# Opening of a fused attention and maxout kernel: weight requests, vector copies and six product units put in another order

## The chip, the cores and the metric

The kernel runs on one core of a Trainium2 chip. The core has engines with a queue of instructions each, worked through in order: TensorE (PE, matrix products and transposes; its weight loads are shown as PEld), VectorE (DVE), ScalarE (ACT), GpSimd (POOL) and SyncE (SP), which only requests transfers. Transfers between device memory and on-chip memory run on 16 DMA engines; here SyncE and GpSimd request nearly all of them, and a request of GpSimd may convert fp32 to bf16 on the way. An engine waits for another one through semaphores. The metric is device time in microseconds of one execution; the profile records one execution in detail.

## What is computed

There are B = 8 batches with H = 8 heads, S = 576 tokens and head size D = 64, and 16 beacon keys and values per head that stand ahead of the ordinary ones. Attention is causal on the ordinary keys and open on the beacons:

```
k_all, v_all = concat([beacon_k, k]), concat([beacon_v, v])     # 592 keys
scores = (q @ k_all.T) / sqrt(64), future ordinary keys masked
a = exp(scores - max); a /= a.sum(-1) + 1e-9
x = (a @ v_all) as [4608 tokens, 512]
h = max(x @ w1, x @ w2, x @ w3)          # 512 -> 768
out = h @ w_out                          # 768 -> 512, fp32
```

## The kernel before, in words

**Attention.** Two heads make a pair; a batch has four pairs, so there are 32 pairs, 0 to 31. Two pairs make a quad. For each pair the queries and keys are turned by TensorE transposes (`turn`, L399, `turn_part`, L417) and copied from PSUM to `qT` and `kT`. Then a burst of score products follows (`emit_scores`, L488, or `emit_burst`, L522), in four groups; ScalarE takes the exponential of each group into `at_sb`. Masks set the future to zero: `emit_masks` (L540) does it on GpSimd (L553), or, with a third argument True, on VectorE (L551), by a product with the triangle `tri`. Then the products with the values and with a column of ones are formed per quad (`emit_pv`, L576, or `emit_pv_whole`, L616), the row sums are inverted on ScalarE (logarithm and exponential) and VectorE multiplies them in, which gives `xT` (L681 or L658), the transposed input of the second part.

**Maxout and output product.** Tokens are taken in 9 blocks of 512. The list `units` (L800 to L818) holds the work of all blocks in order. For the first block the products with w1 and w2 are twelve half units (`mm1_halves`, L733: two column tiles, 256 tokens), and those with w3 six units of 512 tokens (`mm1_unit`, L722). Then four output units follow (`mm2_unit`, L756). A unit whose entry is larger than `ready` may not be emitted yet: the half units of tokens 0 to 255 need nothing but the first half of batch 0, those of tokens 256 to 511 the rest of it. The copy or maximum behind a unit runs on VectorE (L754, L752, L729), or in part on ScalarE where a unit closes a stage. `F(n)` in the opening emits the next n units.

**What sets the order.** The whole order is written out by hand under a manual schedule: each call appends to the queues of the engines that it uses. `start` and `first_batch` (L910) write out batch 0, whose pairs are handled in halves of 288 tokens, `second_batch` (L998) handles pairs 4 to 7 with two or three units between the bursts, and the loop of `emit_all` (L1048) handles pairs 8 to 31. In that loop the number of units emitted by the end of a pair is given as an absolute count (L1054), so units that were not emitted earlier are caught up there.

**PSUM.** There are eight banks. In the first batch they have fixed roles: 0 to 3 for scores, 4 and 5 for turning and for values, 6 and 7 for units. From the turning of pair 4 on, `free_banks` is a list from which the bank that has been used least lately is taken; L992 sets it once.

**Transfers.** The first batch's queries and keys are requested at the start, most of them by GpSimd; its values by SyncE behind a gate, a tiny VectorE write (L291). `cast_first_v(t)`, written `V(t)`, converts the t-th of five value tiles on GpSimd (L332). `load_w(i, gs)` lets GpSimd request halves of weight array i (L342). `load_cast(p)` lets GpSimd request the queries and keys of pairs 4 to 9 (L256). For later batches SyncE requests fp32 data (`load_pair`, L218, `load_v`, L288) and GpSimd converts them (L275, L320); `next_load` takes the next ones of a list.

In `first_batch`, `S_` stands for `emit_scores`, `T` for `turn_part`, `M` for `emit_masks`, `P` for `emit_pv`.

Of the kernel before, what the change touches and what calls it, by code (L numbers as in the profile page):

```python
# [17 lines left out]
def kernel(  # L18
# [22 lines left out]
    n_ft = d_ff // 128  # L41
# [99 lines left out]
    free_banks = list(range(N_BANK))  # L141
# [63 lines left out]
    by_pool = nc.gpsimd.tensor_copy  # L205
# [102 lines left out]
    def cast_v(b, piece, cast):  # L308
        st = stage.pop(("v", b, piece))
        if b not in v_tiles:  # L310
            v_tiles[b] = v_pool.tile([128, n_kt, H, D], BF16, name="v_sb")
        v_sb = v_tiles[b]
        t_lo, t_hi = V_PIECES[piece]
        t = t_lo
        while t < t_hi:
            t1 = t + 1
            while t1 < t_hi and k_rows[t1] == k_rows[t]:
                t1 += 1
            n = k_rows[t]
            cast(  # L320
                v_sb[0:n, t:t1].rearrange("p t h d -> p (t h d)"),
                st[0:n, (t - t_lo) * H * D : (t1 - t_lo) * H * D],
            )
            t = t1
# [14 lines left out]
    def load_w(i, gs=range(n_quad)):  # L339
        wv = (moe_w1, moe_w2, moe_w3)[i].rearrange("(g p e) f -> g p e f", g=n_quad, e=2)  # L340
        for g in gs:
            nc.gpsimd.dma_start(out=w_in[i][:, 2 * g : 2 * g + 2], in_=wv[g])  # L342
# [6 lines left out]
    def load_beacons(b0, b1, dst, queue=None):  # L349
        for b in range(b0, b1):  # L350
            (queue or nc.sync).dma_start(
                out=dst[Nb * (b - b0) : Nb * (b - b0 + 1)],
                in_=beacon_k[b].rearrange("h n d -> n h d"),
            )

    def turn_beacons(b0, b1, src):
        n = Nb * (b1 - b0)
        ps = sc_psum.tile(BF16)[:, 0, 0 : PPB * n].rearrange("p (i n) -> p i n", i=PPB)
        for pi in range(PPB):
            nc.tensor.transpose(  # L360
                ps[:, pi],
                src[:, 2 * pi : 2 * pi + 2].rearrange("p h d -> p (h d)"),
                ident[0:n, 0:n],
            )
        if b0 == 0:
            by_act(kTs[0][:, 0:Nb], ps[:, 0, 0:Nb])
        by_act(bT[:, :, Nb * b0 : Nb * b1], ps)
# [43 lines left out]
    def fill(at_bank, n):  # L411
        for _ in range(n):
            nc.tensor.matmul(  # L413
                acc[:, at_bank], busy[:, 0:128], busy, start=True, stop=True
            )
# [29 lines left out]
    def place_beacons(p, copy):  # L445
        b, pi = divmod(p, PPB)
        copy(kTs[p % NT][:, 0:Nb], bT[:, pi, Nb * b : Nb * (b + 1)])
# [8 lines left out]
    def turn_pair(p, q_copy):  # L456
        banks = [next_psum(BF16)[:, 0:S] for i in range(2)]
        for i in range(2):
            turn(p, i, banks[i])
        evac_k(p, banks[1], by_dve)  # L460
        evac_q(p, banks[0], q_copy)
# [213 lines left out]
    def multiply(count=NPASS):  # L675
        for _ in range(min(count, len(products))):
            quad, hf, n, ps, recip = products.pop(0)
            b, g = divmod(quad, n_quad)
            c0 = b % RING * S + hf * HALF
            part, bank, lo, ca, cb = passes[hf][n]  # L680
            nc.vector.tensor_mul(  # L681
                xT[:, 2 * g + part - 1, c0 + ca : c0 + cb],
                ps[bank][:, lo : lo + cb - ca],
                recip[:, ca:cb],
            )
            if g == n_quad - 1 and n == NPASS - 1:
                ready[0] = 2 * b + hf
# [8 lines left out]
    MID = TOKB // 2  # L696
# [103 lines left out]
    units = []  # L800
    for tb in range(n_tokb):
        need = 2 * ((TOKB * (tb + 1) - 1) // S) + 1
        if tb == 0:
            order = [(lo, f, i) for i in range(2) for lo in (0, MID) for f in (0, 2, 4)]
            *order, last = order
            for lo, ft, i in order:
                units.append((need if lo else 0, mm1_halves, (tb, ft, i, lo, lo + MID)))
            for ft in range(n_ft):
                units.append((need, mm1_unit, (tb, ft, 2)))
            units.insert(len(order) + 2, (need, mm1_halves, (tb, last[1], last[2], last[0], last[0] + MID)))  # L810
        else:
            for ft in range(n_ft):
                for i in range(3):
                    units.append((need, mm1_unit, (tb, ft, i)))
        for tt in range(TOKB // 128):
            units.append((need, mm2_unit, (tb, tt)))
# [8 lines left out]
    def emit_ffn(limit, new_ps=ffn_psum.tile, close=False):  # L825
        if not may_emit(limit):
            return False
        need, fn, args = units[done[0]]
        done[0] += 1
        fn(*args, new_ps, *([True] if close else []))  # L830
        return True
# [26 lines left out]
    def next_load(n=1, **gate):  # L858
        for _ in range(n):
            if loads:  # L860
                loads.pop(0)(**gate)
# [42 lines left out]
    S_, T, M, P, V = emit_scores, turn_part, emit_masks, emit_pv, cast_first_v  # L904

    def F(n=1, new_ps=ffn_psum.tile, close=False):
        for _ in range(n):
            assert emit_ffn(END, new_ps, close)

    def first_batch():  # L910
        S_(0, 0)
        T(2, 0, 0, 6)
        T(3, 0, 0, 4)
        load_v(0, 0, nc.vector)
        load_v(0, 1)
        load_beacons(1, B_PE, bk32_1)
        S_(1, 0)
        T(2, 0, 1, 7)
        T(3, 0, 1, 5)
        S_(2, 0)  # L920
        T(0, 1, 0, 6, None, 2)
        T(1, 1, 0, 4)
        S_(3, 0)
        M(0, 0, True)
        M(1, 0, True)
        T(0, 1, 1, 7, None, 2)
        T(1, 1, 1, 5)
        S_(0, 1)
        T(2, 1, 0, 6, None, 2)
        T(3, 1, 0, 4)  # L930
        S_(0, 2)
        M(0, 1)
        M(2, 0, True)
        T(2, 1, 1, 7, None, 2)
        T(3, 1, 1, 5)
        S_(0, 3)
        M(0, 2)
        M(3, 0, True)
        S_(1, 1)
        M(0, 3, True)  # L940
        V(0)
        load_w(0, [0])
        fill(6, 2)
        S_(1, 2)
        M(1, 1)
        V(1)
        load_w(0, [1])
        S_(1, 3)
        M(1, 2)
        fill(6, 2)  # L950
        S_(2, 1)
        M(1, 3, True)
        V(2)
        fill(6, 2)
        S_(2, 2)
        M(2, 1)
        V(3)
        S_(2, 3)
        M(2, 2)
        V(4)  # L960
        load_w(1, [0])
        P(0, 0)
        S_(3, 1)
        M(2, 3, True)
        P(1, 0, apart=True)
        S_(3, 2)
        M(3, 1)
        S_(3, 3)
        M(3, 2)
        M(3, 3, True)  # L970
        load_w(1, [1])
        by_pool(bk16_1, bk32_1)
        load_cast(PPB)
        load_cast(PPB + 1)
        load_cast(PPB + 2)
        load_w(2)
        load_cast(PPB + 3)
        invert_sums()
        invert_sums()
        multiply()  # L980
        multiply()
        P(0, 1, tiles=sc_psum.tile())
        invert_sums()
        P(1, 1, tiles=sc_psum.tile())
        multiply()
        invert_sums()
        F(3)
        multiply()
        turn_beacons(1, B_PE, bk16_1)
        place_beacons(PPB, by_act)  # L990
        F(3)
        free_banks[:] = [4, 5, 0, 1, 2, 3, 6, 7]  # L992
        turn_pair(PPB, by_act)
        load_v(1, 0, nc.vector)
        load_v(1, 1)
        F(2, next_psum)

    def second_batch():  # L998
        for p in range(PPB, 2 * PPB):
            place_beacons(p + 1, by_act)  # L1000
            emit_burst(p)
            if p == PPB + 1:
                load_cast(2 * PPB)
            if p == PPB + 2:
                load_w_out()
                load_cast(2 * PPB + 1)
            for gi in range(NG):
                emit_masks(p, gi)
                if p == PPB + 2 and gi == 1:
                    cast_v(1, 0, by_pool)  # L1010
            if p == PPB + 2:
                cast_v(1, 1, by_pool)
                next_load(gate=nc.gpsimd)
                next_load(4)
            if p + 1 < 2 * PPB:
                turn_pair(p + 1, by_dve)
                F(2, next_psum)
                if p < PPB + 2:
                    F(1, last_pair(), True)
        F(2, next_psum)  # L1020
        finish = emit_pv_whole(n_quad)
        turn_pair(2 * PPB, by_dve)
        F(2, next_psum)
        finish()
# [93 lines left out]
```

## Time and profile before

| quantity | value |
| --- | --- |
| median of 3 runs | 288.97 us (288.5 to 290.31) |
| the profiled execution | 288.44 us |
| its span, first to last instruction | 286.7 us |
| granted TensorE clock, mean | 0.997 |
| busy: TensorE, VectorE, ScalarE, GpSimd | 274.8, 173.7, 160.0, 135.7 us |
| DMA traffic | 48.84 MB, mean 170 GB/s |

The times of the views count from the start of the span. A row of a timeline gives start and length of one or several equal instructions, the engine, the source line, the operation with target and source, shape and count; brackets hold the idle time of the engine before it and who ended it. Matmuls are pipelined, so several in a row take less than the sum of their single lengths. Some matmul records are missing, so that a count can be one or two short. A list of transfers gives, per request, size and time from request to landing.

### The profile page before, as it was taken

To read this page: it belongs to the slowest core of one execution; us is meant where nothing else is said; L and a number is where in the kernel's file an instruction comes from. 1 tells how busy PE (TensorE), PEld (TensorE's weight loads), DVE (VectorE), ACT (ScalarE), POOL (GpSimd) and SP (SyncE) were. 2 spreads that over 40 slices of the span, in tenths; PEclk is the share of its full clock that TensorE was granted. 3 is DMA by queue.
4 is the path that set the end of the run, shared out by engine and by line. 5 is a ranking of instruction groups with operands and counts; after the bars stand their busy time and mean duration, and the time that the engine had idled before them with its cause. 6 is when DMAs were issued, how large, how long until landed. Compare 5 with 4: busy or idle time off the path is not lost.

```text
span 286.7 us, 7740 instructions
## 1 busy us (share of the span) xinstructions
PE 274.8 (96%) x3042; PEld 156.9 (55%) x3073; DVE 173.7 (61%) x306; ACT 160.0 (56%) x299; POOL 135.7 (47%) x282
## 2 busy tenths in 40 slices
PE   7789899998999999999999999999999999999994
PEld 3447675554556555555556787455555554444442
DVE  4757776554683848373836383648363847876872
ACT  3796287698568595858585757666666640000000
POOL 7088269368477683648465836484436210000000
PEclk9999999999999999999999999999999999999998
DMA  8999999999994899999999999989853003003004
GB/s 142 201 153 140 207 208 170 246 200 313 268 188 127 236 267 195 184 234 257 260 209 202 245 237 242 196 177 232 179 139 114 0 2 133 16 1 146 2 0 146
DMA packets 85316, 48.84 MB, mean 170 GB/s; under 512 B 64416, under 2 KB 80032, under 8 KB 85280
## 3 DMA queue, kind: packets, MB, share of 16 engines
q1 hardware_dynamic: 78176, 42.22, 64.3%
q0 software_dynamic: 6544, 5.80, 13.8%
q8 instruction: 24, 0.39, 0.6%
q10 hardware_dynamic: 560, 0.33, 0.5%
q14 instruction: 12, 0.10, 0.2%
HBM read 35.13 MB, written 14.22 MB: 172 GB/s over the span
## 4 chain that ended last, share of the span: by engine, by line
PE 89%; DVE 3%; ACT 2%; POOL 2%; issue 1%; DMA 1%; SPq 0%; ACTq 0%; DVEq 0%
PE acc L711 44%; PE acc L763 16%; PE acc L635 11%; PE acc L513 8%; PE acc L740 4%; PE acc L602 2%; PE acc L404 2%; PE acc L466 1%; DMA out_dram<-y 1%; ACT at_sb L507 1%; PE acc L498 1%; POOL v_sb L320 1%; ACT at_sb L531 1%; PE acc L413 1%; PE acc L425 1%
## 5 line engine op out<-in xcount | busy, mean ns | idle before, releaser
L711 PE MATMUL acc<-xT,w_sb 128*128 128x512 bf16 (+4 forms) x720 | 134.5, 337 | 2.0 <-DVE xT L658 0.4
L553 POOL TENSOR_SCALAR_AFFINE_SELECT at_sb<-at_sb 128x256 bf16<-128x256 bf16 (+2 forms) x176 | 63.7, 383 | 91.4 <-ACT at_sb L531 80.4
L729 DVE TENSOR_TENSOR hT<-hT,acc 128x512 bf16<-128x512 bf16 x102 | 70.0, 687 | 59.6 <-PE acc L711 56.4
L711 PEld LDWEIGHTS <-w_sb 128*128 128x128 bf16 x744 | 69.1, 98 | 59.4 <-issue 0.2
L531 ACT ACTIVATE at_sb<-acc 128x208 bf16<-128x208 f32 (+3 forms) x140 | 89.6, 735 | 8.5 <-PE acc L513 7.3
L763 PE MATMUL acc<-w_out_sb,hT 128*128 128x512 bf16 (+2 forms) x241 | 48.2, 348 | 0.3
L275 POOL CAST p<-st 96x768 bf16<-96x768 f32 x44 | 35.0, 824 | 0.0
L763 PEld LDWEIGHTS <-hT 128*128 128x128 bf16 x246 | 22.6, 98 | 22.2 <-DVE hT L729 1.9
L770 DVE COPY y<-acc 128x512 f32<-128x512 f32 (+1 forms) x35 | 22.0, 628 | 20.9 <-PE acc L763 14.0
L731 ACT CAST hT<-acc 128x352 bf16<-128x352 f32 x18 | 8.1, 452 | 45.8 <-PE acc L711 45.8
L731 DVE CAST hT<-acc 128x512 bf16<-128x512 f32 (+1 forms) x48 | 26.6, 554 | 10.0 <-PE acc L711 9.8
L513 PE MATMUL acc<-qT,kT 64*128 64x208 bf16 (+1 forms) x336 | 26.7, 279 | 0.1
L788 ACT COPY y<-acc 128x320 f32<-128x320 f32 x1 | 0.4, 426 | 46.0 <-PE acc L781 46.0
L635 PE MATMUL acc<-at_sb,v_sb 128*32 128x512 bf16 (+5 forms) x672 | 23.0, 281 | 0.6 <-POOL v_sb L320 0.6
L513 PEld LDWEIGHTS <-kT 64*128 64x128 bf16 x336 | 15.2, 94 | 12.5 <-issue 2.6
L658 DVE TENSOR_TENSOR xT<-raw,recip 128x576 bf16<-128x576 f32 x28 | 21.1, 796 | 0.0
L635 PEld LDWEIGHTS <-v_sb 128*32 128x32 bf16 (+1 forms) x672 | 14.5, 96 | 7.8 <-POOL v_sb L320 1.2
L320 POOL CAST v_sb<-st 128x1536 bf16<-128x1536 f32 (+2 forms) x21 | 18.3, 896 | 0.0
L645 ACT COPY raw<-acc 128x512 f32<-128x512 f32 x28 | 15.8, 630 | 2.6 <-PE acc L635 2.3
L635 PE MATMUL acc<-at_sb,ones 128*32 128x512 bf16 (+3 forms) x336 | 14.9, 283 | 0.0
L507 ACT ACTIVATE at_sb<-acc 128x1024 bf16<-128x1024 f32 (+3 forms) x16 | 13.1, 864 | 3.3 <-PE acc L498 3.1
L740 PE MATMUL acc<-xT,w_sb 128*128 128x256 bf16 x96 | 11.8, 272 | 0.8 <-DVE xT L681 0.8
(73 smaller groups left out, 176.8 us busy)
## 6 DMA issues: line engine op xcount, KB each, us to landing
out_dram<-y SPq DMA_DIRECT2D x35, 256.0 KB, 3.5
st<-in_q_dram SPq DMA_DIRECT2D x22, 288.0 KB, 4.4
st<-in_k_dram SPq DMA_DIRECT2D x22, 288.0 KB, 5.0
st<-in_v_dram SPq DMA_DIRECT2D x24, 256.0 KB, 5.9
w_sb<-in_moe_w_dram POOLq DMA_DIRECT2D x6, 384.0 KB, 6.9
q_dram<-p SPq DMA_DIRECT2D x16, 144.0 KB, 2.3
k_dram<-p SPq DMA_DIRECT2D x16, 144.0 KB, 2.2
st<-in_v_dram SPq DMA_DIRECT2D x8, 224.0 KB, 5.8
```

The source lines that it names most:

```text
L275: cast(t16.rearrange("p r h d -> p h r d"), st[0:QP, i * NQ2 : (i + 1) * NQ2].rearrange("p (h r d) -> p h r d", h=2, r=QR),)
L320: cast(v_sb[0:n, t:t1].rearrange("p t h d -> p (t h d)"), st[0:n, (t - t_lo) * H * D : (t1 - t_lo) * H * D],)
L513: nc.tensor.matmul(ps, kTs[p % NT][hs, 128 * t : 128 * t + 128], qTs[p % NT][hs, q0:q1], start=True, stop=True, tile_position=(64 * e, 0),)
L531: nc.scalar.activation(out=both_heads(p, gi)[:, e0:e1], in_=acc[:, first + e0 : first + e1, 0 : g_width(p, gi)], func=AF.Exp, scale=scale,)
L553: nc.gpsimd.affine_select(out=view, in_=view, compare_op=ALU.is_ge, fill=0.0, base=x0, pattern=[[0, 2], [1, hi - lo]], channel_multiplier=-1,)
L635: nc.tensor.matmul(acc[32 * j : 32 * j + 32, bank, lo + q0 - qa : lo + qb - qa], lhsT, at_view(PPQ * quad + j // 2, t, j % 2, q0, qb), sta ...
L711: nc.tensor.matmul(ps[:, a:b], w_in[i][:, ct, 128 * ft : 128 * (ft + 1)], xT[:, ct, x0 : x0 + b - a], start=(ct == 0), stop=(ct == n_ct - 1),)
L729: nc.vector.tensor_max(h[:, lo:hi], h[:, lo:hi], ps[:, lo:hi])
L731: (by_act if hi < TOKB else by_dve)(h[:, lo:hi], ps[:, lo:hi])
L740: nc.tensor.matmul(ps, w_in[i][:, ct, 128 * (ft + f) : 128 * (ft + f + 1)], xT[:, ct, tb * TOKB + lo : tb * TOKB + hi], start=(ct == 0), s ...
L763: nc.tensor.matmul(ps[:, lo:hi], hT[:, ft, 128 * tt : 128 * (tt + 1)], w_out_sb[:, ft, lo:hi], start=(ft == 0), stop=(ft == n_ft - 1),)
L770: (by_act if hi < d_model else by_dve)(y[:, lo:hi], ps[:, lo:hi])
```

## The change

It edits three places. In `units`, the twelfth half unit is no longer moved behind two w3 units; the twelve stand in order. In `first_batch`, VectorE's masks of pairs 0, 1 and 2 (group 0) move behind the copies of the next transposes; the first four weight requests move ahead of their former places among GpSimd's masks and casts, the first one ahead of `V(0)`, and `V(0)` itself ahead of mask (0, 2); VectorE's multiplication of the second quad's second half follows one unit instead of three, pair 4 is turned behind five units instead of six, and one unit instead of two follows it. `free_banks` has its last two entries exchanged. So two units fewer have been emitted when pair 4's burst begins, and the absolute count in the loop catches them up at pair 9. In `second_batch`, five loads of SyncE, with their gate on GpSimd, move ahead of the second value cast of batch 1.

```diff
@@ units @@
         if tb == 0:
-            order = [(lo, f, i) for i in range(2) for lo in (0, MID) for f in (0, 2, 4)]
-            *order, last = order
-            for lo, ft, i in order:
-                units.append((need if lo else 0, mm1_halves, (tb, ft, i, lo, lo + MID)))
+            for i in range(2):
+                for n, lo in ((0, 0), (need, MID)):
+                    for ft in range(0, n_ft, 2):
+                        units.append((n, mm1_halves, (tb, ft, i, lo, lo + MID)))
             for ft in range(n_ft):
                 units.append((need, mm1_unit, (tb, ft, 2)))
-            units.insert(len(order) + 2, (need, mm1_halves, (tb, last[1], last[2], last[0], last[0] + MID)))
@@ first_batch @@
         S_(3, 0)
-        M(0, 0, True)
-        M(1, 0, True)
         T(0, 1, 1, 7, None, 2)
         T(1, 1, 1, 5)
         S_(0, 1)
+        M(0, 0, True)
         T(2, 1, 0, 6, None, 2)
         T(3, 1, 0, 4)
         S_(0, 2)
         M(0, 1)
-        M(2, 0, True)
+        load_w(0, [0])
+        M(1, 0, True)
         T(2, 1, 1, 7, None, 2)
         T(3, 1, 1, 5)
         S_(0, 3)
+        V(0)
         M(0, 2)
+        load_w(0, [1])
+        M(2, 0, True)
         M(3, 0, True)
         S_(1, 1)
         M(0, 3, True)
-        V(0)
-        load_w(0, [0])
         fill(6, 2)
         S_(1, 2)
         M(1, 1)
         V(1)
-        load_w(0, [1])
         S_(1, 3)
         M(1, 2)
+        load_w(1, [0])
         fill(6, 2)
...
         S_(2, 2)
         M(2, 1)
+        load_w(1, [1])
         V(3)
         S_(2, 3)
         M(2, 2)
         V(4)
-        load_w(1, [0])
...
         M(3, 3, True)
-        load_w(1, [1])
         by_pool(bk16_1, bk32_1)
...
         invert_sums()
-        F(3)
+        F()
         multiply()
+        F(2)
         turn_beacons(1, B_PE, bk16_1)
         place_beacons(PPB, by_act)
-        F(3)
-        free_banks[:] = [4, 5, 0, 1, 2, 3, 6, 7]
+        F(2)
+        free_banks[:] = [4, 5, 0, 1, 2, 3, 7, 6]
         turn_pair(PPB, by_act)
         load_v(1, 0, nc.vector)
         load_v(1, 1)
-        F(2, next_psum)
+        F(1, next_psum)
@@ second_batch @@
             if p == PPB + 2:
-                cast_v(1, 1, by_pool)
                 next_load(gate=nc.gpsimd)
                 next_load(4)
+                cast_v(1, 1, by_pool)
```

## The prediction

> **What bounds the kernel now.** I read the busy shares of the page first, then the gaps of TensorE in its timeline, then what stood before each gap on the other engines, and last the landings of the transfers.
>
> ```profile
> PE 274.8 (96%) x3042; PEld 156.9 (55%) x3073; DVE 173.7 (61%) x306; ACT 160.0 (56%) x299; POOL 135.7 (47%) x282
> ```
>
> TensorE is busy 274.8 of 286.7 us; no other engine passes 61%. Where its 11.9 us of idle time lie decides what an edit can win. One stretch of the view by windows (time, then busy us of PE, PEld, DVE, ACT, POOL, clock, DMA share, GB/s):
>
> ```profile
> 75.00:240.00 165.00, 163.97 (x1789) 95.71 (x1807) 96.27 (x153) 106.89 (x203) 88.68 (x180) 1.00 0.84 187
> ```
>
> From 75 to 240 us TensorE lacks 1.03 us in 165 and has the full clock. So a microsecond won or lost before 75 us goes straight to the end; the change edits only that part. The rows of TensorE's timeline there on which I rest (start, length, line, count, in brackets the idle time before and who ended it):
>
> ```profile
> 11.08 0.45 PE L425 MATMUL acc<-ident,quad 96*64 96x96 bf16 x12
> ...
> 12.46 0.26 PE L498 MATMUL acc<-qT,kT 64*128 64x208 bf16 x2 [0.70 <-DVE kT L433]
> ...
> 19.15 0.40 PE L602 MATMUL acc<-at_sb,ones 128*32 128x288 bf16 x12
> ...
> 22.25 0.68 PE L602 MATMUL acc<-at_sb,ones 128*32 128x288 bf16 x20 [0.54 <-ACT at_sb L507]
> ...
> 25.36 2.86 PE L740 MATMUL acc<-xT,w_sb 128*128 128x256 bf16 x24
> ...
> 28.36 0.39 PE L740 MATMUL acc<-xT,w_sb 128*128 128x256 bf16 x2
> ...
> 29.37 0.27 PE L740 MATMUL acc<-xT,w_sb 128*128 128x256 bf16 x1 [0.62 <-DVE xT L681]
> 29.80 2.52 PE L740 MATMUL acc<-xT,w_sb 128*128 128x256 bf16 x21 [0.16 <-DVE xT L681]
> ...
> 32.25 0.70 PE L404 MATMUL acc<-ident,quad 96*64 96x96 bf16 x24
> ...
> 53.39 2.76 PE L763 MATMUL acc<-w_out_sb,hT 128*128 128x512 bf16 x11
> ...
> 65.02 0.38 PE L711 MATMUL acc<-xT,w_sb 128*128 128x512 bf16 x1 [0.42 <-DVE xT L658]
> ...
> 70.49 0.83 PE L635 MATMUL acc<-at_sb,v_sb 128*32 128x512 bf16 x16 [0.33 <-POOL v_sb L320]
> ...
> 71.61 0.90 PE L635 MATMUL acc<-at_sb,v_sb 80*32 80x80 bf16 x24 [0.29 <-POOL v_sb L320]
> ```
>
> Four places: VectorE's key copy (0.70), VectorE's xT product (0.62 + 0.16), xT of the second batch (0.42), and GpSimd's value casts (0.33 + 0.29). No gap names a weight: unit 0 starts at 25.36 without one.
>
> **The change part by part.** *VectorE's copies ahead of the masks.*
>
> ```profile
> 10.94 1.09 DVE L551 TENSOR_TENSOR at_sb<-at_sb,tri 128x224 bf16<-128x224 bf16 x6
> 11.95 0.82 DVE L433 COPY kT<-acc 128x288 bf16<-128x288 bf16 x2
> ...
> 26.45 0.69 DVE L754 CAST hT<-acc 128x512 bf16<-128x512 f32 x1
> ...
> 28.26 0.69 DVE L754 CAST hT<-acc 128x512 bf16<-128x512 f32 x1 [0.25 <-PE acc L740]
> ...
> 28.87 0.88 DVE L681 TENSOR_TENSOR xT<-acc,recip 128x288 bf16<-128x288 f32 x3
> ...
> 54.24 0.75 DVE L440 COPY qT<-acc 128x576 bf16<-128x576 bf16 x1
> ```
>
> Six masks (1.09 us) stand before the key copy for which TensorE waits at 12.46. With the copies first, pair 0's can start when the first six of the twelve transposes of 11.08 are in: about 11.4, at the latest 11.53. It takes about 0.45 (two take 0.82), so TensorE resumes near 11.95: **0.5 us** won (0.4 to 0.7). The masks move behind into idle time of VectorE; the first is read by the value products at 19.15, so they cost nothing, unless VectorE were full there, and then 1.09 at most. The 0.5 carries on, since ScalarE's exponentials run gapless in the middle of the opening:
>
> ```profile
> 15.09 5.00 ACT L507 ACTIVATE at_sb<-acc 128x576 bf16<-128x576 f32 x7 [0.36 <-PE acc L498]
> ...
> 25.94 0.44 ACT L671 ACTIVATE recip<-recip 128x288 f32<-128x288 f32 x1
> ```
>
> Their first one waits for TensorE (0.36), so all seven start earlier with it. Their pace remains a floor: the 0.54 at 22.25 stays.
>
> *Weights between masks and casts.* The rows of GpSimd's timeline; then the landings (last number, us from issue) of the first and the fourth half of the first two weight arrays, of the last tile of the first values, and of pair 4's keys; then the DMA load (last two numbers) in two windows:
>
> ```profile
> 13.83 0.40 POOL L553 TENSOR_SCALAR_AFFINE_SELECT at_sb<-at_sb 128x256 bf16<-128x256 bf16 x1 [7.86 <-ACT at_sb L507]
> ...
> 15.62 0.57 POOL L342 DMA_DIRECT2D w_sb<-in_moe_w_dram  x1
> ...
> 18.46 0.68 POOL L332 CAST v_sb<-st 128x512 bf16<-128x512 f32 x1
> ...
> 22.54 0.55 POOL L342 DMA_DIRECT2D w_sb<-in_moe_w_dram  x1
> ```
>
> ```profile
> w_sb<-in_moe_w_dram POOLq DMA_DIRECT2D x1, 384.0 KB, 4.7
> ...
> w_sb<-in_moe_w_dram POOLq DMA_DIRECT2D x1, 384.0 KB, 7.7
> ...
> st<-in_v_dram SPq DMA_DIRECT2D x1, 160.0 KB, 5.2
> ...
> quad<-in_k_dram POOLq DMA_DIRECT2D x1, 144.0 KB, 7.2
> ```
>
> ```profile
> 15.00:16.00 1.00, 1.00 (x12) 0.38 (x7) 1.00 (x5) 0.92 (x2) 1.00 (x3) 1.00 0.84 181
> 16.00:17.00 1.00, 0.45 (x7) 0.19 (x4) 0.28 (x3) 1.00 (x2) 0.48 (x2) 1.00 0.78 113
> ```
>
> The first request moves from 15.62 to behind the mask of 13.83 (itself 0.5 earlier): about 13.7, so 1.9 us sooner. The others follow among the casts. TensorE waited for no weight, so they win nothing themselves. But the halves land one behind another: the first at 15.62 + 4.7 = 20.3, the fourth at 22.54 + 7.7 = 30.2, three steps of 3.3; and pair 4's keys, issued at 24.3, land right behind at 31.5. An earlier start moves the keys too: by 0 if the weights find no room beside the values, by 1.9 if they find it all. From 15 to 17 the DMA engines show 0.84 and 0.78, part of it free, so I take **1.1**, just over the middle: keys at 30.4. Three of the four requests (0.57 each) now stand before the third value cast, of 18.46, instead of two: with everything else 0.5 earlier that cast ends near 18.6 to 18.7. TensorE's value products start at 19.15 - 0.5 = 18.65 with the sums (0.40) and read it after them: hidden by these 0.4; without that cover, up to 0.57.
>
> *Five units ahead of pair 4, VectorE's product after the first unit.* Unit 3 of the first products needs xT of the second half of the tokens. ScalarE had its reciprocal at 26.38 (25.94 + 0.44), but VectorE put three casts of finished units before the three products of 28.87. From 28.36 to 32.32 units 3 to 5 take 3.96 us where units 0 to 2 took 2.86 (row of 25.36): 1.1 lost. Afterwards the products follow the first cast (26.45 + 0.69), end about 0.9 later, at 28.0 on the old scale, and unit 3 finds them done. What is late next: unit 3 needs the bank of unit 1, whose cast now ends at 28.0 + 0.69 = 28.7 against a start at 28.4. That is 0.3 lost, net **0.8 us** (0.3 to 1.1).
>
> Pair 4 is then turned at 32.25 - 0.95 (one unit, 2.86/3) - 0.5 - 0.8 = 30.0; the keys are read 0.35 later, at 30.35, and land at 30.4: **0.1 lost** (0 to 1.1). The burst of pair 4 follows after one unit; the key copy (as large as the 0.75 of 54.24) fits beside that unit's 0.95.
>
> *Two units later in the order from here.* The bursts of pairs 4 to 7 start two units earlier relative to the units, which costs TensorE nothing by itself. From pair 8 on the difference is two output units; eleven recorded matmuls of twelve take 2.76 at 53.39, so 2.8 us. They now stand between the bursts of pairs 9 and 10. So xT of the second batch is asked for 2.8 later after its product: the 0.42 of 65.02 goes. GpSimd's work behind the burst of pair 9 runs without a gap into the value casts:
>
> ```profile
> 67.43 1.59 POOL L275 CAST p<-st 96x768 bf16<-96x768 f32 x2
> 68.97 2.58 POOL L320 CAST v_sb<-st 128x1536 bf16<-128x1536 f32 x3
> ```
>
> With 2.8 us more between burst and use, they end before they are needed: 0.33 + 0.29 go. Together **1.0 us** (0 to 1.04). New: before the burst of pair 8 stand two first-layer units (0.95 each) instead of two output units, and VectorE, which turns pair 8's queries until 54.99 (54.24 + 0.75), casts them late; the last group of the burst needs the second one's bank: **0.2 lost** (0 to 0.5). The next loads moved ahead of the second value cast on GpSimd are asked for 1.2 us sooner relative to the casts and never waited for: 0 (0.3 either way).
>
> The sum: 0.5 + 0.8 - 0.1 + 1.0 - 0.2 = **2.0 us**. The profiled execution took 288.44 (span 286.7 and 1.7 around it): 286.4 by its scale. It lies 0.5 below the median of the runs shown, 288.97; the forecast for the median is 288.97 - 2.0 = **287.0**.
>
> **The rivals.** *Pair 4's keys take the place of the wait.* If the weights get no room beside the values, the keys still land at 31.5 and TensorE stands 1.1 at pair 4. For it: they land at a fixed place behind the weights, and TensorE comes 2.25 sooner. Against: the shares of 0.84 and 0.78. The gain shrinks by 1.05: 288.0.
>
> *The weights push out the last values (slower).* Which of two queues the DMA engines serve (packets, MB, share of 16 engines; q1 carries SyncE's requests, q0 GpSimd's): the microsecond from 13, that from 18, and that from 36, after a request of SyncE:
>
> ```profile
> q1 hardware_dynamic: 788, 0.20, 104.1%
> ...
> q0 software_dynamic: 63, 0.19, 100.4%
> ...
> q0 software_dynamic: 213, 0.20, 123.4%
> ...
> 33.81 0.31 SPq L299 DMA_DIRECT2D st<-in_beacon_v_dram  x1
> ```
>
> From 13 only values flow, 1.041 x 16 / 788 = 21 ns of an engine per packet; from 18 only weights, 255 ns each. The 0.84 of the window from 15 are then about 640 packets of values, 40 per engine, the last tile's, which was asked for at 12.5 and landed 5.2 later at 17.7. If an engine took one packet of each queue in turn, they would take 40 x 0.276 = 11 us while weights last (four times 3.3): landing near 26, cast near 26.7. TensorE wants it about 0.9 after 22.25 - 0.5, so 4.0 late; the gains past there (and the 0.1 at pair 4) stay: 288.97 - 2.0 - 0.1 + 4.0 = 290.9. It bites from a landing later than 22 and makes the kernel slower from 24. Against: the values asked for from 33.81 have no packet from 36 to 37, where 213 of q0, asked for earlier, are all that these two queues move. That looks like order of request, and this tile is asked for before the weights.
>
> [...]
>
> *It doesn't do what it says later.* The waits of 65.02 and 70.49 return at other places because the loads of the second batch are no sooner while TensorE is: gain 1.0, so 288.0.
>
> **How the numbers follow.** Forecast 0.63, keys late 0.14, later waits return 0.14, values pushed out 0.09. All terms at their best end (0.7 + 1.1 + 1.04 + 0.3) give 3.1 less: 285.8; both rivals of 288.0 together give 289.0. With a few tenths for the spread of a median the range is 285.6 to 289.3; the slower rival lies beyond it. About 1% (2.9 us) is what a measurement of this kernel can tell from no change: faster than that needs every term at its best (0.09), slower needs the slower rival at a third more than its price of 4.0 and little gained (0.06), within 0.85.
>
> **What would show it.** Right: TensorE's row of about 12.46 waits 0.2 or less; no wait of the first products for xT L681 and a short one for hT L754; pair 4's transposes start at about 30 and wait for their keys 0.3 at most; no wait for xT L658 or v_sb L320 near 65 and 70. Wrong: a TensorE or GpSimd wait for st between 18 and 23, a wait for the quad before pair 4 above 0.5, or 75 us on no longer gapless.

## The result, and the profile after

The changed kernel took 287.43 us in the median of eight runs (286.45 to 287.76), the kernel before 288.97 (288.5 to 290.31): the ratio is 0.9937, with the 95% interval 0.9916 to 0.9958. The forecast was 287.0, 2.0 less than before; 1.5 less were measured. The profiled execution took 286.92 with a span of 285.2, against 288.44 and 286.7. So the size is nearly that of the forecast, but the way to it is not: what stands ahead of the burst of pair 9 was to win 1.0 and lost 0.3, and what stands from there on was to win 1.0 and won 1.7.

The page of the changed kernel, its busy shares:

```profile
PE 275.9 (97%) x3073; PEld 157.4 (55%) x3073; DVE 176.6 (62%) x306; ACT 160.1 (56%) x299; POOL 136.5 (48%) x282
```

The long middle is as gapless as before, so that what happens ahead of 75 us still goes straight to the end (view by windows, columns as in the prediction):

```profile
75.00:240.00 165.00, 165.00 (x1809) 95.78 (x1808) 96.35 (x153) 106.67 (x201) 88.84 (x180) 1.00 0.87 187
```

TensorE's timeline of the changed kernel, the rows that answer to those of before:

```profile
12.16 0.26 PE L498 MATMUL acc<-qT,kT 64*128 64x208 bf16 x2 [0.20 <-DVE kT L433]
...
20.79 0.20 PE L602 MATMUL acc<-at_sb,ones 128*32 128x48 bf16 x2 [0.45 <-DVE at_sb L551]
...
22.58 0.68 PE L602 MATMUL acc<-at_sb,ones 128*32 128x288 bf16 x20 [0.76 <-ACT at_sb L507]
...
25.19 0.22 PE L602 MATMUL acc<-at_sb,ones 80*32 80x80 bf16 x4 [0.46 <-issue]
...
26.34 2.86 PE L740 MATMUL acc<-xT,w_sb 128*128 128x256 bf16 x24
...
29.57 1.91 PE L740 MATMUL acc<-xT,w_sb 128*128 128x256 bf16 x16 [0.16 <-DVE hT L754]
31.40 0.70 PE L404 MATMUL acc<-ident,quad 96*64 96x96 bf16 x24
...
33.87 0.38 PE L513 MATMUL acc<-qT,kT 64*128 64x336 bf16 x6 [0.17 <-DVE hT L754]
...
54.54 0.36 PE L513 MATMUL acc<-qT,kT 64*128 64x336 bf16 x5 [0.20 <-DVE hT L729]
...
60.53 0.92 PE L513 MATMUL acc<-qT,kT 64*128 64x208 bf16 x12
...
68.06 0.92 PE L513 MATMUL acc<-qT,kT 64*128 64x208 bf16 x12
...
71.16 1.04 PE L711 MATMUL acc<-xT,w_sb 128*128 128x512 bf16 x4
```

The wait for the key copy fell from 0.70 to 0.20, and yet unit 0 starts at 26.34 instead of 25.36. Three waits stand between that were not forecast: one for a mask of VectorE (0.45), a longer one for ScalarE (0.76 instead of 0.54), and one for nothing that the profile shows ("issue", 0.46). Not all of the 0.98 belongs to the change. VectorE's copy of the queries that precedes all that was edited starts 0.20 later too (VectorE's timeline, the kernel before and the changed one):

```profile
10.20 0.82 DVE L433 COPY qT<-acc 128x288 bf16<-128x288 bf16 x2 [0.84 <-PE acc L425]
...
10.40 0.82 DVE L433 COPY qT<-acc 128x288 bf16<-128x288 bf16 x2 [0.84 <-PE acc L425]
```

Such shifts differ from one execution to the next: this copy starts between 10.08 and 10.72 in the profiles of this case. Counted from it, unit 0 starts after 15.16 before and after 15.94 now, 0.78 later. From unit 0 to the turning of pair 4 the forecast holds. The points of the kernel before that the rest is compared with, from its timeline:

```profile
56.09 1.21 PE L513 MATMUL acc<-qT,kT 64*128 64x208 bf16 x12
...
62.93 0.92 PE L513 MATMUL acc<-qT,kT 64*128 64x208 bf16 x12
...
68.45 0.91 PE L513 MATMUL acc<-qT,kT 64*128 64x208 bf16 x12
...
72.53 1.04 PE L711 MATMUL acc<-xT,w_sb 128*128 128x512 bf16 x3
```

The burst of pair 9 (burst 9, at 62.93 before) starts 2.40 earlier, at 60.53, but the two output units that stood ahead of it are still to come. Two such units take 2.70 in the kernel before, from 53.39 (in the prediction) to the next row, burst 8 at 56.09. So the changed kernel is 0.3 behind here, 0.2 of it from the later start. From burst 9 to burst 10 (68.06, before 68.45) it needs 7.53 us instead of 5.52 with those 2.7 more in it: 0.7 won. From burst 10 to the unit after the value products it needs 3.10 instead of 4.08: 1.0 won. That makes 1.4 at 71.16, and the spans differ by 1.5.

### The profile page after: what moved, and what is told of

It reads as the page before. It is cut to its first block, busy times and chain, and to the rows that moved or that the text cites. A ratio compares the mean times of both kernels' runs of the same rounds, so it can differ in the third digit from the quotient of the medians.

```text
span 285.2 us, 7775 instructions
## 1 busy us (share of the span) xinstructions
PE 275.9 (97%) x3073; PEld 157.4 (55%) x3073; DVE 176.6 (62%) x306; ACT 160.1 (56%) x299; POOL 136.5 (48%) x282
## 4 chain that ended last, share of the span: by engine, by line
PE 91%; DVE 5%; ACT 1%; issue 1%; ACTq 0%; DVEq 0%
PE acc L711 46%; PE acc L763 16%; PE acc L635 11%; PE acc L513 8%; PE acc L740 3%; DVE at_sb L551 2%; PE acc L404 2%; PE acc L466 2%; PE acc L602 1%; ACT at_sb L531 1%; DVE kT L433 1%; DVE hT L754 1%; PE acc L425 1%; DVE qT L433 1%; PE acc L413 1%
## 5 line engine op out<-in xcount | busy, mean ns | idle before, releaser
L553 POOL TENSOR_SCALAR_AFFINE_SELECT at_sb<-at_sb 128x256 bf16<-128x256 bf16 (+2 forms) x176 | 64.5, 387 | 92.0 <-ACT at_sb L531 81.7
L763 PEld LDWEIGHTS <-hT 128*128 128x128 bf16 x246 | 22.6, 98 | 21.7 <-DVE hT L729 1.6
L451 DVE COPY kT<-acc 128x576 bf16<-128x576 bf16 x12 | 9.0, 753 | 5.7 <-PE acc L404 5.7
```

What stands on the lines that cost most here:

```text
L553: nc.gpsimd.affine_select(out=view, in_=view, compare_op=ALU.is_ge, fill=0.0, base=x0, pattern=[[0, 2], [1, hi - lo]], channel_multiplier=-1,)
L763: nc.tensor.matmul(ps[:, lo:hi], hT[:, ft, 128 * tt : 128 * (tt + 1)], w_out_sb[:, ft, lo:hi], start=(ft == 0), stop=(ft == n_ft - 1),)
```

## The experiments

Two theories of the late unit 0 stood after this profile. **Masks:** the masks, moved behind the copies, hold up VectorE, and the value products wait for them. **Weights:** the early weight requests delay something that TensorE needs, and the mask wait only hides it. Each experiment is told with its edit against the changed kernel, unless another one is named. The medians of the kernel before were 288.97 beside the first four kernels, 288.85 beside the next four and 289.0 beside the last four.

### 1. All masks of VectorE's first group ahead

```diff
         S_(0, 1)
         M(0, 0, True)
+        M(1, 0, True)
+        M(2, 0, True)
+        M(3, 0, True)
         T(2, 1, 0, 6, None, 2)
...
-        M(1, 0, True)
...
-        M(2, 0, True)
-        M(3, 0, True)
```

> The changed kernel with VectorE's masks of pairs 1, 2 and 3 (group 0) directly behind that of pair 0, ahead of the copies of pairs 2 and 3. Theory (VectorE's masks are held up while GpSimd works without a gap): all four run from 12.4 to about 15, mostly before GpSimd starts at 13.5; no mask above 0.8 us, the mask of 2.28 us is gone, TensorE's wait for at_sb L551 near 20.8 too, unit 0 starts at 25.0 to 25.3 instead of 26.34, and the time falls by 1.0 to 1.3 us below the changed kernel, to about 286.3. Rival (the late start of unit 0 comes from the 0.46 us without a named releaser at 25.2 and from ScalarE's pace, not from the masks): unit 0 stays at 25.9 or later and the time falls by 0.4 at most.

It took 287.37 us, ratio 0.9936 (0.9914 to 0.9958): nothing gained over the changed kernel. The masks became short, as expected: twelve of them take 2.10 in one row of VectorE, where nine of them took 5.63 in the changed kernel. The wait for a mask is gone.

```profile
12.59 2.10 DVE L551 TENSOR_TENSOR at_sb<-at_sb,tri 128x224 bf16<-128x224 bf16 x12
...
16.22 5.63 DVE L551 TENSOR_TENSOR at_sb<-at_sb,tri 128x224 bf16<-128x224 bf16 x9
```

TensorE's timeline of this kernel:

```profile
25.49 0.22 PE L602 MATMUL acc<-at_sb,ones 80*32 80x80 bf16 x4 [1.19 <-issue]
...
26.65 2.87 PE L740 MATMUL acc<-xT,w_sb 128*128 128x256 bf16 x24
```

The unnamed wait grew to 1.19 and unit 0 stayed late, at 26.65. So the masks were delayed, but they do not set unit 0: the theory of the masks fell.

### 2. Weights and the first value cast at their old places

```diff
         M(0, 1)
-        load_w(0, [0])
...
-        V(0)
         M(0, 2)
-        load_w(0, [1])
...
         M(0, 3, True)
+        V(0)
+        load_w(0, [0])
...
         V(1)
+        load_w(0, [1])
...
-        load_w(1, [0])
...
-        load_w(1, [1])
...
         V(4)
+        load_w(1, [0])
...
         M(3, 3, True)
+        load_w(1, [1])
```

> The changed kernel with the four weight requests and V(0) at their places of before; masks stay late. Theory (any gapless work of GpSimd holds the masks up): GpSimd is still gapless from 16.7 to 21 with casts and masks, so the longest mask stays above 1 us and unit 0 at 25.8 or later; pair 4's keys land at 31 to 31.5 and cost TensorE 0 to 0.5; the time is 0 to 0.5 above the changed kernel. Rival (it is the requests that hold the masks up): no mask above 0.5, unit 0 near 25.0, pair 4 waits about 1 us for its keys, and the time is 0 to 0.4 below the changed kernel.

It took 288.41, ratio 0.9976 (0.993 to 1.0022), which can't be told from the kernel before. The opening is as forecast for the change (TensorE's timeline):

```profile
12.37 0.26 PE L498 MATMUL acc<-qT,kT 64*128 64x208 bf16 x2 [0.20 <-DVE kT L433]
...
25.28 2.86 PE L740 MATMUL acc<-xT,w_sb 128*128 128x256 bf16 x24
...
30.70 0.45 PE L404 MATMUL acc<-ident,quad 96*64 96x96 bf16 x12 [0.30 <-DMA quad<-in_q_dram]
31.43 0.45 PE L404 MATMUL acc<-ident,quad 96*64 96x96 bf16 x12 [0.28 <-DMA quad<-in_k_dram]
...
51.45 0.90 PE L635 MATMUL acc<-at_sb,v_sb 80*32 80x80 bf16 x24 [1.36 <-POOL v_sb L320]
```

There is no unnamed wait. Unit 0 is at 25.28, 14.66 after the copy of the queries: the 0.50 of the key copies arrives in full. The masks of the first group are short although they stand where the change put them (seven take 1.26 in one row). Two waits came instead. The queries and keys of pair 4 are late by 0.30 and 0.28: the rival of the keys, at half its price. And the last value tile of the second batch is late by 1.36 at 51.45, which no theory had. The runs spread from 286.53 to 290.01.

### 3. Masks at their old places, weights early

```diff
         S_(3, 0)
+        M(0, 0, True)
+        M(1, 0, True)
         T(0, 1, 1, 7, None, 2)
...
-        M(0, 0, True)
...
-        M(1, 0, True)
+        M(2, 0, True)
...
-        M(2, 0, True)
```

> The changed kernel with VectorE's masks of pairs 0 to 3 (group 0) at their places of before, ahead of the key copies; weights and units as changed. Theory: the 0.70 us wait for kT at about 12.5 returns, the long masks go, unit 0 starts at 25.3 to 25.5 and unit 3 has no wait for xT, so the time is 0.8 to 1.0 below the changed kernel, about 286.5. Rival (the masks' place matters by the key copy alone): the time is 0.3 above the changed kernel.

It took 287.73, ratio 0.9948 (0.9919 to 0.9977). The 0.70 for the key copy is back, the unnamed wait is 1.10 at 26.00, and unit 0 starts at 27.16 instead of the expected 25.3 to 25.5, the latest so far. So unit 0 is late with early weights whatever the masks do. Some masks are still long, although they stand where they stood before: six take 4.52 us in one row of VectorE.

### 4. Only the units, the turning and the swap of loads

Against the kernel before: the hunks of the change in `units` and `second_batch`, and in `first_batch` this one.

```diff
-        F(3)
+        F()
         multiply()
+        F(2)
         turn_beacons(1, B_PE, bk16_1)
         place_beacons(PPB, by_act)
-        F(3)
-        free_banks[:] = [4, 5, 0, 1, 2, 3, 6, 7]
+        F(2)
+        free_banks[:] = [4, 5, 0, 1, 2, 3, 7, 6]
...
-        F(2, next_psum)
+        F(1, next_psum)
```

> The kernel before with the units' part of the change alone: five units ahead of pair 4, the product after the first unit, the loads ahead of the second value cast; masks and weight requests as before. Forecast: unit 0 at 25.36, no wait for xT at unit 3 (0.8 won), the later waits for xT and v_sb gone (1.0 won), pair 4's keys landing at 31.5 where they are asked for at 30.8 (0.4 to 0.9 lost), 0.35 lost at the bursts of pairs 4 and 8: about 0.8 below the kernel before, 288.1. If instead the keys came without a wait, 287.4.

It took 287.92, ratio 0.9958 (0.9922 to 0.9994), with a spread from 286.43 to 290.65. The time is near the forecast 288.1, but not by its terms: the expected wait for pair 4's keys is absent, with the weights at their old places. Its profiled execution was the longest of the ten, and its TensorE timeline shows why:

```profile
52.42 0.91 PE L635 MATMUL acc<-at_sb,v_sb 80*32 80x80 bf16 x24 [2.87 <-POOL v_sb L320]
```

This is the wait of 51.45 of the second experiment, at its largest. The list of transfers of this kernel, for the requests from 41.2 to 42 us (size, then us to landing):

```profile
w_out_sb<-in_moe_w_out_dram POOLq DMA_DIRECT2D x1, 768.0 KB, 9.2
...
st<-in_v_dram SPq DMA_DIRECT2D x1, 160.0 KB, 10.7
```

The last value tile lands 10.7 us after its request, beside 768 KB of `w_out`. In the changed kernel it took 7.0 and no wait followed. The view by windows of this kernel shows a lower granted clock (third last number) in the stretch of the wait and in the next one; it is 1.00 in the ten microseconds ahead of them, and 0.994 in the mean of the execution:

```profile
50.00:55.00 5.00, 2.36 (x62) 1.64 (x64) 0.82 (x2) 2.18 (x6) 2.43 (x7) 0.89 1.14 254
55.00:60.00 5.00, 4.97 (x62) 2.05 (x64) 3.52 (x5) 2.66 (x6) 1.38 (x2) 0.77 1.27 203
```

### 5. The first experiment with the second weight array at its old places

Against the kernel of the first experiment:

```diff
-        load_w(1, [0])
...
-        load_w(1, [1])
...
         V(4)
+        load_w(1, [0])
...
         M(3, 3, True)
+        load_w(1, [1])
```

> The changed kernel with the masks of pairs 1 to 3 directly behind pair 0's (as in the first experiment) and the two halves of w1 requested where they were before; w0's two halves stay early. Theory (TensorE's block of instructions is fetched through the same DMA engines, behind the weights that were asked for before it): the 16 KB instruction packet near 21 to 23 starts about 1.5 us sooner than in the first experiment (23.11), the unnamed wait of 1.19 at 25.5 is gone, unit 0 starts at 25.0 to 25.4 instead of 26.65. The time is 1.2 below the first experiment, about 286.2, unless batch 1's last value tile falls behind w_out in the DMA queues; then TensorE waits 1 to 3 for v_sb near 50 and the time is 287.2 or more. Rival (the wait at 25.5 is due to something in the value product, not to the fetch): it stays, 0.4 or more, and unit 0 is at 26 or later.

It took 286.13, ratio 0.9913 (0.9887 to 0.994), the fastest median of all. Unit 0:

```profile
24.91 2.86 PE L740 MATMUL acc<-xT,w_sb 128*128 128x256 bf16 x24
```

This is nearly the start that was forecast for the change (24.85), 14.66 after the copy of the queries, without any unnamed wait, although the halves of the first array are still early.

### 6. The same with the request of `w_out` behind a value cast

Against the kernel of the fifth:

```diff
             if p == PPB + 2:
-                load_w_out()
                 load_cast(2 * PPB + 1)
...
                     cast_v(1, 0, by_pool)
+                    load_w_out()
```

> The kernel of e5 with w_out requested behind the first value cast of batch 1 instead of ahead of pair 6's masks. Theory (the last value tile of batch 1 is late only where w_out, 768 KB, stands ahead of it): no wait for v_sb near 50, the last tile lands by 46.5, and the time is 286.0 to 286.4, whether or not e5 had the wait. Rival (the values are late because TensorE comes earlier): the wait stays.

It took 286.23, ratio 0.9918 (0.9894 to 0.9941), from 285.63 to 286.95 in four runs, a narrower spread than that of the fifth's ten (285.54 to 288.52). The wait for the last value tile is absent, as it was in the fifth's profile. But an unnamed wait of 0.69 came back in the opening, where the edit changes nothing:

```profile
24.76 0.22 PE L602 MATMUL acc<-at_sb,ones 80*32 80x80 bf16 x4 [0.69 <-issue]
```

### 7. Eight more instructions ahead on TensorE

```diff
     def start():
-        keep_busy(8, 480)
+        keep_busy(16, 240)
```

> The changed kernel with the eight filling products of 480 columns at the very start split into sixteen of 240 columns: eight more instruction pairs, the same work and time. Theory (a block of instructions arrives late): the unnamed wait of the second value product moves by eight products, from before the seventeenth product with the ones (80 rows) to before the ninth, and keeps its time, TensorE going on about 2.4 us after the start of the 16 KB instruction packet. Rival (that product itself waits for something): the wait stays before the seventeenth.

Twice as many idle products of half the length stand at the start, so that every later instruction of TensorE has a number eight products higher. It took 287.89 in one execution. TensorE's timeline:

```profile
23.12 0.43 PE L602 MATMUL acc<-at_sb,ones 128*32 128x288 bf16 x8
25.46 0.43 PE L602 MATMUL acc<-at_sb,ones 128*32 128x288 bf16 x12 [1.91 <-DVE xT L681]
```

In the changed kernel the wait stood behind 16 products with the ones of this group; here it stands behind 8. It moved by exactly the eight that were added, so it belongs to a place in the instruction stream and not to any data. (The name of the releaser in the bracket is inferred; a wait that moves by eight products against the data is no wait for `xT`.)

What is late there is in the queue view (packets, MB, share of 16 engines), here for the changed kernel, first over the whole execution, then in the 0.1 us from 22.7:

```profile
q8 instruction: 24, 0.39, 0.6%
...
q8 instruction: 1, 0.02, 60.9%
```

The 24 packets hold 16 KB each. TensorE's 3073 products and 3073 weight loads make 6146 instructions, which is 256 for each packet if these carry nothing else. One of these packets moves just then. Where TensorE waited, it resumed 2.2 to 2.4 us after that packet began: after 22.76 at 25.19 in the changed kernel, after 23.11 at 25.49 in the first experiment, after 23.67 at 26.00 in the third, after 22.44 at 24.76 in the sixth, after 23.16 at 25.46 here. The others with that wait (experiments 8 to 11) lie in the same range. Where it did not wait, the packet had begun at 21.0 to 21.7 (before, and experiments 2, 4, 5 and 12). That TensorE waits for this packet is the author's reading: the view calls the queue instruction, the wait of 0.46 to 1.91 us keeps its place in the stream, and its end follows the packet's start at nearly the same distance.

An unnamed wait near a later packet stands in three of the profiles: 0.70 in experiment 1 and 0.31 in experiment 12, both ahead of the fifth of the six products of an output unit, and 0.33 here. TensorE's timeline, experiment 1 and this one:

```profile
59.14 0.60 PE L763 MATMUL acc<-w_out_sb,hT 128*128 128x512 bf16 x2 [0.70 <-issue]
...
57.92 0.21 PE L635 MATMUL acc<-at_sb,v_sb 128*32 128x64 bf16 x4 [0.33 <-issue]
58.07 1.47 PE L763 MATMUL acc<-w_out_sb,hT 128*128 128x512 bf16 x5
```

Here the wait stands ahead of the last four value products before that unit, which is again eight products sooner.

### 8. The fourth experiment with `w_out` behind a value cast

Against the kernel of the fourth: the edit of the sixth.

> The kernel of the fourth experiment (units' part alone, weights and masks as before) with w_out requested behind the first value cast of batch 1. Theory: the wait for v_sb near 52 (2.87) disappears, TensorE's clock stays at 1.00 between 40 and 60, and the time falls to 286.4 to 286.9, so that the early weights of the change are worth nothing but this order. Rival: the wait stays above 1 us and the time at 287.5 or more.

It took 286.86, ratio 0.9926 (0.9892 to 0.9961). The 2.87 is gone and the spread is 286.28 to 288.23 in nine runs, which fits with `w_out` as its cause; how the two transfers share the engines stands under experiment 12. Without the early weights and the moved masks this kernel is no slower than the changed one (0.9937). The opening again shows something unforeseen:

```profile
25.76 0.22 PE L602 MATMUL acc<-at_sb,ones 80*32 80x80 bf16 x4 [1.18 <-issue]
```

Here all weights are at the places of the kernel before, and the packet of instructions still begins late, at 23.53. So early weights are not the only thing that makes it late.

### 9. Only the weights and the first value cast early

Against the kernel before: the hunks of the second experiment, reversed.

> The kernel before with the weight requests and the first value cast at the places of the change, and nothing else. Theory (early weights delay TensorE's instruction packet and here win nothing, since no transfer was waited for): the 16 KB packet starts at 22.7 to 23.7 instead of 21.5, an unnamed wait of 0.4 to 1.2 stands before the seventeenth product with the ones near 25.5, unit 0 starts at 26 to 26.7 and the time is 0.5 to 1.2 above the kernel before. Rival (the packet comes late by chance and not because of the weights): unit 0 at 25.4 and the time within 0.3 of the kernel before.

It took 289.82, ratio 1.0025 (1.0005 to 1.0046): this part alone makes the kernel 0.8 slower in the medians, 0.05 to 0.46% by the interval. The packet begins at 23.92, the unnamed wait is the second longest, and unit 0 is at 27.47, all three beyond what was expected:

```profile
26.32 0.22 PE L602 MATMUL acc<-at_sb,ones 80*32 80x80 bf16 x4 [1.73 <-issue]
```

One open end belongs here. Of the 78 runs of the kernel before, 50 took 288.2 to 289.2 us, 25 took 289.7 to 290.6 and three more than that; the ten of this kernel lie from 289.1 to 290.7. A packet that is late in a third of the executions of the kernel before would make such a second group. No run shows that it is so, for the one profiled execution of that kernel took 288.44.

### 10 and 11. The loads swapped back, and the changed kernel again

```diff
             if p == PPB + 2:
+                cast_v(1, 1, by_pool)
                 next_load(gate=nc.gpsimd)
                 next_load(4)
-                cast_v(1, 1, by_pool)
```

> The changed kernel with the five loads behind the second value cast of batch 1 again. Forecast: nothing, within 0.3 of the changed kernel, no wait for v_sb or the turned pair near 60 to 72. Rival (the earlier loads are what removes the later waits): 0.3 to 0.6 us of waits for v_sb near 70 come back.

> The changed kernel once more, for a comparison with the next one on the same chip: 287.2 to 287.7, with the unnamed wait before unit 0 between 0.3 and 1.2 us.

The two took 287.19 (ratio 0.9928, 0.99 to 0.9955) and 287.2 (0.9936, 0.9914 to 0.9958): the swap is worth nothing, as forecast. This second profile of the changed kernel has no wait for a mask and an unnamed wait of 1.64, more than the 1.2 allowed for, with unit 0 at 26.96; the first had both kinds. So of the two, the unnamed wait is the constant one.

### 12. The fifth again

> The kernel of e5 once more beside the changed kernel: 1.0 to 1.4 below it where the instruction packet comes by 21.5, no better where it comes at 22.5; median 286.0 to 286.5.

It took 286.75, ratio 0.994 (0.9908 to 0.9973), above the expected 286.0 to 286.5 and only 0.45 below the changed kernel. Unit 0 is at 25.04 without a wait, as in the fifth. But the profiled execution has the value wait, which the fifth had not, and a span of 287.0 instead of 283.8:

```profile
51.45 0.91 PE L635 MATMUL acc<-at_sb,v_sb 80*32 80x80 bf16 x24 [2.45 <-POOL v_sb L320]
```

The last value tile was asked for at 40.09 and `w_out` at 40.74, and the tile landed at 50.73; in the fifth it landed at 46.09. The queue view of the microsecond from 46 (q0 carries `w_out`, q1 the values; first this profile, then that of the fifth, which has no line for q1):

```profile
q0 software_dynamic: 146, 0.15, 92.1%
q1 hardware_dynamic: 138, 0.04, 26.6%
...
q0 software_dynamic: 205, 0.21, 125.6%
```

Here the rest of the values moves beside `w_out`; there they were through before. The same pair of kernels shows two groups of times: 15 of 22 runs took 285.5 to 287.0 us, seven 287.5 to 289.7. In the sixth, with `w_out` requested later, all four runs lie in the lower group, but with a share of 15 in 22 that would happen by chance about one time in five, so it is not shown that the upper group is gone. It has the best median without a high run, 286.2 us, 0.8% under the kernel before. Its interval and that of the changed kernel in experiment 11 overlap, so the 1.0 us between their medians is not shown to be more than noise.

## Why the prediction was right or wrong

- **Key copies ahead of masks, 0.5: right.** The wait at the key copy went from 0.70 to 0.20. Where the packet of instructions began by 21.7, the whole 0.5 arrives at unit 0: it starts 14.66 after the copy of the queries in experiments 2, 5 and 12, and 15.16 after it before.
- **"The masks cost nothing": wrong in this step, though covered.** Their time was taken as 0.18 each (1.09 for six) from a row in which they ran ahead of GpSimd's first mask, at 13.83. In the changed kernel nine of them take 5.63 us in one row of VectorE, and TensorE waited 0.45 for one and 0.22 longer for the next exponential. Unit 0 would have been late without these waits too, as experiment 1 shows.
- **The weights "win nothing themselves": the step that failed.** Their cost was looked for in data that lands late (values, keys). What came late was a packet of instructions, which began at 22.76 instead of 21.51. This term is absent from the sum. Counted from the copy of the queries, unit 0 starts 1.3 to 2.1 later with both arrays early than with the same masks and no such wait (15.94 to 16.75 against 14.66, and 16.44 and 17.07 against 15.16). It turned the 0.5 won into 0.8 lost. Experiments 1, 3, 9 and 11 show it with early weights and whatever masks; 5 and 12 lose it with only the second array's two requests moved back. That the early requests are what delays the packet is not fully shown: in experiment 6 it was late, at 22.44, with the first array alone early, in experiment 8, at 23.53, with none.
- **Product after the first unit, 0.8: right, 0.9 measured.** From unit 0 to the turning of pair 4 the changed kernel needs 31.40 - 26.34 = 5.06; before it was 32.25 - 0.95 - 25.36 = 5.94. The short wait for hT L754 was forecast at 0.3 and is 0.16.
- **Keys, -0.1: 0.** No wait stands at 31.40. The bound of 1.9 was the shift of the first request alone; the last weight request moved from 22.54 to 19.23, and the keys landed at 27.9 instead of 30.4. The rival of the late keys was real in one of the runs without early weights: experiment 2 pays 0.58, experiment 4 nothing.
- **Later waits, 1.0: right in place, too small.** 0.42 and 0.33 + 0.29 went, as forecast, but 0.7 and 1.0 were won. The brackets count the idle time alone; work that overlapped without the wait follows one after the other with it. Ahead of the wait of 70.49 the row of 69.29, 0.87 long, needs 1.20 us to the next one, in the changed kernel 0.70, an overlap of 0.17: 0.50 for a bracket of 0.33. The prediction took two output units as 2.8; in its own timeline the row that follows them starts 2.70 after their 53.39. The short wait ahead of burst 8 is 0.20, as forecast, but a like one of 0.17 in the burst of pair 4 was missed.
- **Rivals.** The values were not pushed out: the last tile of the first values landed 5.5 us after its request, before it was 5.2. So no run shows the 4.0 that the rival put on them, an estimate from one packet of each queue in turn; where both queues moved, q0 and q1 had 55 and 42 packets in the microsecond from 16 of the changed kernel, 146 and 138 in that from 46 of experiment 12. The prediction held against that rival that transfers are served in the order of request; in experiment 12 a tile asked for 0.65 ahead of `w_out` moved beside it and landed 10.6 after its request. The later waits did not return in the changed kernel; in experiments 2, 4 and 12 one does, in another place and by another cause than that rival had, a value tile late beside `w_out`.
- **What would show it.** One of the signs for a right forecast failed: pair 4 was turned at 31.40, not at about 30. None of the signs for a wrong one points at a packet of instructions.

By the steps: ahead of burst 9, 1.0 forecast and -0.3 measured; behind it, 1.0 and 1.7. The errors of 1.3 and 0.7 have opposite signs. That the total came out near is luck.

## What to carry to other kernels

A transfer that no line of the kernel asks for can be late, and here it was late each time both weight arrays were requested early (its start between 22.76 and 23.92, against 21.51 before): look for packets of instructions in the queue view, and at an unnamed wait add a few instructions ahead of it and see whether it moves by as many. When a forecast comes out right, hold each term against its own place in the trace; here two wrong terms made a right sum. Times counted from the start of the span carry a shift between executions (up to 0.64 us here), so count from a row that the edit can't reach. A large load with a distant use, like `w_out` here, belongs behind small ones that are needed soon: in all three profiles with a late value tile (TensorE waited 1.36, 2.87 and 2.45 us), that tile moved beside `w_out`.

## What the runs showed of the hardware

- The unnamed wait of TensorE near 25, 0.46 to 1.91 us long, moved by eight products when eight more stood ahead of it (experiment 7). It ended 2.2 to 2.4 us after the start of a 16 KB packet of the queue that the view calls instruction, those near 59 ended 2.6 to 3.0 after the start of such a packet. What sets the packet's start stays open: it was late in all seven profiles with both arrays early (22.76 to 23.92), but also in two of the seven with the second array at its old places (experiments 6 and 8, at 22.44 and 23.53), whose openings are those of 5 and 4, where it began by 21.7.
- A mask of 128x256 took 0.28 us on VectorE in experiment 2 and up to 2.28 in the changed kernel's first profile. There the longest began at 17.55 and ended at 19.83, while GpSimd worked without a gap (timelines of VectorE and of GpSimd):

```profile
17.55 2.28 DVE L551 TENSOR_TENSOR at_sb<-at_sb,tri 128x256 bf16<-128x256 bf16 x1
...
17.77 0.55 POOL L342 DMA_DIRECT2D w_sb<-in_moe_w_dram  x1
18.32 0.62 POOL L332 CAST v_sb<-st 128x512 bf16<-128x512 f32 x1
18.88 0.41 POOL L553 TENSOR_SCALAR_AFFINE_SELECT at_sb<-at_sb 128x256 bf16<-128x256 bf16 x1
19.23 0.55 POOL L342 DMA_DIRECT2D w_sb<-in_moe_w_dram  x1
```

  In experiment 7, beside the same casts and requests, the masks from 13.7 to 16.1 took 0.19 to 0.34, and one at 17.26 took 1.30, so that what decides is not shown here.
- One idle time of 2.87 us of TensorE was followed by a mean granted clock of 0.77 in the five microseconds from 55 (experiment 4); after the one of 2.45 in experiment 12 the clock stayed at 1.00 until 65.
